# Value preparation on GpSimd per pair of heads, and row-tiled warm-up matmuls, in a fused hash-attention and MLP kernel

## Chip, cores, metric

One core of a Trainium2 chip. The metric is the device time of one launch in microseconds (us). The span of a profile is about 1.8 us shorter than the time of the same run.

## The reference, cut to what matters

```python
def _attn_ref(q, k, v, proj):            # q, k, v: (4, 8, 768, 64)
    q_bits = einsum('bhsd,dk->bhsk', q, proj) > 0      # 6 bits; k_bits likewise
    mask = q_bucket[:, :, :, None] == k_bucket[:, :, None, :]
    scores = where(mask, scale * q @ k.T, -1e9)
    attn = softmax(scores)
    return attn @ v
def _moe_ref(x, w_in, w_out):            # x: (3072, 512), d_ff 2048
    h = x @ w_in
    return (h / (1 + exp(-h))) @ w_out   # silu
```

The kernel does 32 heads in pairs (16 pairs), with 9 score units of 128x512 for each head, and weaves the MLP of a finished batch between later score units.

## The kernel before: the parts concerned

V of each head is cast to float16 (`vv`), and the sum of its six row blocks is made (`vs`). In the first eight heads (and the last) a matmul of `dmat` against `vs` starts the head's output, and the products with `vv` follow; the other heads use `vs` four score units later. A pair's q and k are cast by GpSimd into `qka` (even head) and `qkb` (odd head). `plan(w, fn)` puts work ahead of score unit `w`, in the order of the calls.

```python
    def warm_up(n):
        for _ in range(n):
            nc.tensor.matmul(wps, warm, warm[:, None, :].to_broadcast([P, 4, P]),
                             start=True, stop=True)
    warm_up(5)
    ...                                                   # cut
    def v_unit(p, heads=(0, 1)):
        for i in heads:
            h = 2 * p + i
            vv, vs = VV[h % NVS], VS[p % (NVS // 2)]
            src = v_sb[p][:, i, :].rearrange("p (t d) -> p t d", d=D)
            nc.gpsimd.tensor_copy(out=vv[:, :, 0:D], in_=src)
            sa = nrm.tile([P, 3, D], F32, tag="vsa", name="vsa")
            nc.gpsimd.tensor_tensor(out=sa, in0=src[:, 0:3], in1=src[:, 3:6], op=ALU.add)
            sb = nrm.tile([P, D], F32, tag="vsb", name="vsb")
            nc.gpsimd.tensor_tensor(out=sb, in0=sa[:, 0], in1=sa[:, 1], op=ALU.add)
            nc.gpsimd.tensor_tensor(out=vs[:, i, 0:D], in0=sb, in1=sa[:, 2], op=ALU.add)
    ...                                                   # cut
        # first unit of a head, where direct(h): the first eight heads and the last
            nc.tensor.matmul(o_ps[h][:, 0:NJ, :], dmat,
                             vs[:, None, :].to_broadcast([P, NJ, E1]), start=True, stop=True)
    ...                                                   # cut: start-up
    t_first(0, 0, nc.scalar.copy)             # q_row: TensorE transposes, copy
    t_first(0, 1, nc.vector.tensor_copy)      # k_row
    warm_up(2)
    bt = proj_first(0)                        # projection, bits
    v_unit(0, (0,))
    ...                                                   # cut: casts, bits
    t_first(1, 0, nc.scalar.copy)
    t_first(1, 1, nc.vector.tensor_copy)
    warm_up(3)
    ...                                                   # cut: then the first scores
    for i in range(2):
        plan(8, lambda i=i: cast_unit(1, i))
        plan(8, lambda i=i: v_unit(1, (i,)))
```

The softmax here doesn't subtract the row's maximum and nothing guards it: scores larger than these inputs give would overflow.

Of the kernel before, what the change touches and what calls it, by code (L numbers as in the profile page):

```python
# [9 lines left out]
F32 = mybir.dt.float32  # L10
F16 = mybir.dt.float16
BF16 = mybir.dt.bfloat16
AF = mybir.ActivationFunctionType
ALU = mybir.AluOpType
# [3 lines left out]
def kernel(  # L18
# [10 lines left out]
    nc = tc.nc  # L29
    B, H, S, D = q.shape  # L30
# [3 lines left out]
    P = 128  # L34
    NJ = S // P
# [4 lines left out]
    E1 = D + 1  # L40
# [6 lines left out]
    cst = ctx.enter_context(tc.tile_pool(name="cst", bufs=1))  # L47
# [5 lines left out]
    nrm = ctx.enter_context(tc.tile_pool(name="nrm", bufs=2))  # L53
# [4 lines left out]
    ps = ctx.enter_context(tc.tile_pool(name="ps", bufs=1, space=bass.MemoryType.PSUM))  # L58
# [5 lines left out]
    v_sb = {}  # L64
# [48 lines left out]
    warm = cst.tile([P, P], BF16, name="warm")  # L113
# [7 lines left out]
    wps = ps.tile([P, 4, P], F32, tag="o", name="warm_ps", bufs=2)  # L121

    def warm_up(n):
        for _ in range(n):
            nc.tensor.matmul(wps, warm, warm[:, None, :].to_broadcast([P, 4, P]),
                             start=True, stop=True)

    warm_up(5)
    ident = cst.tile([P, P], F32, name="ident")
    make_identity(nc, ident)  # L130

# [17 lines left out]
    NSL = 4  # L149
    QKA = [cst.tile([P, 2 * S], F16, name=f"qka{i}") for i in range(NSL)]  # L150
    QKB = [cst.tile([P, 2 * S], F16, name=f"qkb{i}") for i in range(NSL)]
    NVS = 8
    VV = [cst.tile([P, NJ, E1], F16, name=f"vv{i}") for i in range(NVS)]
    VS = [cst.tile([P, 2, E1], F16, name=f"vs{i}") for i in range(NVS // 2)]
    for i in range(NVS):
        nc.vector.memset(VV[i][:, :, D:E1], 1.0)
        nc.vector.memset(VS[i // 2][:, i % 2, D:E1], float(NJ))
    for i in range(NSL):
        (nc.vector if i < 2 else nc.gpsimd).memset(QKB[i][0:64, :], 0.0)
    ident16 = cst.tile([P, P], F16, name="ident16")  # L160
# [46 lines left out]
    def cast_first(h, n, e, eng):  # L207
        dst = halves(QKA[0], slice(0, D), n, e) if h == 0 else \
            halves(QKB[0], slice(D, 2 * D), n, e)
        x0 = (2 * h + n) * HS  # L210
        src = qk32[0][e * D : (e + 1) * D, x0 : x0 + HS].rearrange("d (x c) -> d x c", c=P)
        if eng is nc.scalar:
            eng.mul(dst, src, CS)
        else:
            eng.tensor_scalar(out=dst, in0=src, scalar1=CS, scalar2=1.0,
                              op0=ALU.mult, op1=ALU.mult)

    def proj_first(h):

        bp = ps.tile([P, 512], F32, tag="m", name="bp_ps", bufs=3)  # L220
        for c in range(4):
            e, n = divmod(c, 2)
            x0 = (2 * h + n) * HS
            o = e * (NBIT + 1)
            nc.tensor.matmul(bp[32 * c : 32 * c + 32, 0:HS], pw[:, o : o + 32],
                             qk32[0][:, x0 : x0 + HS], start=True, stop=True)
        bt = btp.tile([P, S], F16, tag="bits", name="bits")
        nc.vector.tensor_scalar(out=bt[:, 0:HS], in0=bp[:, 0:HS],
                                scalar1=sc[:, 0:1], scalar2=sc[:, 1:2],
                                op0=ALU.is_gt, op1=ALU.subtract)  # L230
        return bt
# [20 lines left out]
                                scalar1=CS, scalar2=1.0,  # L252
                                op0=ALU.mult, op1=ALU.mult)

    def v_unit(p, heads=(0, 1)):
        for i in heads:
            h = 2 * p + i
            vv, vs = VV[h % NVS], VS[p % (NVS // 2)]
            src = v_sb[p][:, i, :].rearrange("p (t d) -> p t d", d=D)
            nc.gpsimd.tensor_copy(out=vv[:, :, 0:D], in_=src)  # L260
            sa = nrm.tile([P, 3, D], F32, tag="vsa", name="vsa")
            nc.gpsimd.tensor_tensor(out=sa, in0=src[:, 0:3], in1=src[:, 3:6], op=ALU.add)  # L262
            sb = nrm.tile([P, D], F32, tag="vsb", name="vsb")
            nc.gpsimd.tensor_tensor(out=sb, in0=sa[:, 0], in1=sa[:, 1], op=ALU.add)
            nc.gpsimd.tensor_tensor(out=vs[:, i, 0:D], in0=sb, in1=sa[:, 2], op=ALU.add)

    bits = {}
    CB = 256
# [83 lines left out]
    def parts(w):  # L352
        h, r = divmod(w, NU)
        jp, j = divmod(r, 3)
        if j == 1:
            return h, [(2 * jp, 512, 256, 0), (2 * jp + 1, 512, 256, 256)]
        return h, [(2 * jp + j // 2, 0, 512, 0)]
# [17 lines left out]
    def direct(h):  # L375


        return h < H or h == B * H - 1

    def av(w):  # L380
        h, pts = parts(w)
        vv, vs = VV[h % NVS], VS[h // 2 % (NVS // 2)][:, h % 2, :]
        if w % NU == 0:
            o_ps[h] = ps.tile([P, NJ + 1, E1], F32, tag="o", name="o_ps", bufs=2)



            if direct(h):
                nc.tensor.matmul(o_ps[h][:, 0:NJ, :], dmat,  # L389
                                 vs[:, None, :].to_broadcast([P, NJ, E1]),  # L390
                                 start=True, stop=True)
        if w % NU == 4 and not direct(h):
            nc.tensor.matmul(o_ps[h][:, NJ, :], dmat, vs,
                             start=False, stop=True, skip_group_check=True)
        u = ut.pop(w)
        for jt, c0, n, o0 in pts:
            for i in range(n // P):
                nc.tensor.matmul(o_ps[h][:, c0 // P + i, :],  # L398
                                 u[:, o0 + i * P : o0 + (i + 1) * P], vv[:, jt, :],
                                 start=(not direct(h) and w % NU == 0 and i == 0), stop=True,  # L400
                                 skip_group_check=True)
        if w % NU == NU - 1:
            o = o_ps.pop(h)
            p, par = divmod(h, 2)
            if par == 0:
                x_pr[p] = xpl.tile([P, NJ, P], F16, tag="xpr", name="x_pr", bufs=4)
            if not direct(h):

                osum = nrm.tile([P, NJ, E1], F32, tag="osum", name="osum")
                vsum = nrm.tile([P, 1, E1], F32, tag="vsum", name="vsum")  # L410
                nc.vector.tensor_copy(out=vsum, in_=o[:, NJ : NJ + 1, :])
                nc.vector.tensor_tensor(  # L412
                    out=osum, in0=o[:, 0:NJ, :], in1=vsum.to_broadcast([P, NJ, E1]),
                    op=ALU.add)
                o = osum
            rec = nrm.tile([P, NJ], F32, tag="rec", name="rec")
            nc.vector.reciprocal(out=rec, in_=o[:, 0:NJ, D])  # L417
            (nc.vector if direct(h) else nc.gpsimd).tensor_tensor(  # L418
                out=x_pr[p][:, :, par * D : (par + 1) * D], in0=o[:, 0:NJ, 0:D],
                in1=rec[:, :, None].to_broadcast([P, NJ, D]), op=ALU.mult)  # L420
# [124 lines left out]
    t_first(0, 1, nc.vector.tensor_copy)  # L545
    warm_up(2)
    bt = proj_first(0)
    v_unit(0, (0,))
    for e in range(2):
        for n in range(2):  # L550
            cast_first(0, n, e, nc.scalar)
# [10 lines left out]
    def second_head():  # L562
        bt = proj_first(1)
        for e in range(2):
            for n in range(2):
                cast_first(1, n, e, nc.gpsimd)
                bits_first(bt, 1, n, e, nc.vector.tensor_copy)
        v_unit(0, (1,))

    at = {}  # L570

    def plan(w, fn):
        at.setdefault(w, []).append(fn)
# [4 lines left out]
        plan(4 + 2 * i, lambda i=i: t_unit(1, i))  # L578
    for i in range(2):
        plan(8, lambda i=i: cast_unit(1, i))  # L580
        plan(8, lambda i=i: v_unit(1, (i,)))
    plan(10, lambda: proj_halves(1))
    for i in range(2):
        plan(11 + i, lambda i=i: bits_halves(1, i))
# [9 lines left out]
    for i in range(4):  # L594
        plan(29 + i, lambda i=i: bits_unit((2, 3), i // 2, i % 2))
    for i in range(2):
        for j in range(2):
            plan(18 + 9 * i + 2 * j, lambda p=2 + i, j=j: v_unit(p, (j,)))
        plan(21 + i, lambda p=4 + i: load_qk(p))
    for i in range(4):  # L600
        plan((24, 40, 68, 74)[i], lambda i=i: load_w_in(i))
# [7 lines left out]
    for Q in range(2, NQUAD):  # L609
        w0 = (Q - 1) * QST  # L610
        for i in range(4 if Q > 2 else 0):
            w1 = w0 + (5, 9, 12, 15)[i]
            plan(w1, lambda Q=Q, i=i: block_unit(2 * Q + i // 2, i % 2))
            if i % 2:
                for par in range(2):
                    plan(w1, lambda p=2 * Q + i // 2, par=par: cast_unit(p, par))
        wp = w0 + {2: 24, 3: 21}.get(Q, 20)
        plan(wp, lambda Q=Q: proj_unit(2 * Q, 2 * Q + 1))
        for i in range(4):
            plan(wp + {2: i, 3: 2 * i}.get(Q, 0),  # L620
                 lambda Q=Q, i=i: bits_unit((2 * Q, 2 * Q + 1), i // 2, i % 2))
        for i in range(2):
            plan(w0 + 5 + i, lambda p=2 * Q + i: load_v(p))
            for j in range(2):
                plan(w0 + 18 + 9 * i + 2 * j, lambda p=2 * Q + i, j=j: v_unit(p, (j,)))
            if Q + 1 < NQUAD:
                plan(w0 + (28 if Q == 3 else 8) + i, lambda p=2 * Q + 2 + i: load_blocks(p))
    for p in range(NPAIR):
# [11 lines left out]
    for w in range(NW):  # L640
# [9 lines left out]
        n = -(-(len(moeq) - keep) // left) if len(moeq) > keep else 0  # L650
# [6 lines left out]
        if n == 1 and len(moeq) - keep < left and skip:  # L657
            n = 0
# [43 lines left out]
```

## Time and profile before

| | before |
|---|---|
| time, median of the runs beside the changed kernel | 303.59 us (303.19 to 303.80) |
| span of the profile | 301.3 us |
| busy: TensorE, ScalarE, VectorE, GpSimd | 98%, 70%, 60%, 43% |
| first exponential on ScalarE | 8.26 us |
| last eviction's end to the end of the span | 2.5 us |

The prediction shows the page's lines. Two marks are used throughout to compare profiles: when ScalarE's first exponential starts, and how far later exponentials lie behind those of before.

### The profile page before, as it was taken

Reading aid. Unit: us, or ns where it says so; the run is one execution under the profiler, and the core shown is the slowest. Engines: PE = TensorE matmul, PEld = TensorE weight load, DVE = VectorE, ACT = ScalarE, POOL = GpSimd, SP = SyncE. Lnnn points to the kernel's source line nnn. Section 1 sums busy time; section 2 is a strip of 40 time slices with the busy share of each in tenths; the row PEclk is TensorE's granted clock in tenths of the full one; section 3 lists DMA queues with packets and bytes.
Section 4 is the critical chain, followed back from the end, with each engine's and each line's share of the span. In section 5 each row is a group of like instructions: output and inputs, shape, how many; then the busy total and the mean of one; then the engine's idle time right before and its main releaser. Section 6 shows DMA issues by size and latency. Waiting matters only on the chain.

```text
span 301.3 us, 7181 instructions
## 1 busy us (share of the span) xinstructions
PE 296.6 (98%) x2710; PEld 175.1 (58%) x2710; DVE 180.1 (60%) x344; ACT 210.1 (70%) x392; POOL 128.3 (43%) x203
## 2 busy tenths in 40 slices
PE   8999999999999999999999999999999999999996
PEld 3676855545665665555565665555566654446653
DVE  5797938899588355854694434954443443664332
ACT  5987989989886777778876666978977722452200
POOL 7589999388418551935158401755111100000000
PEclk9999999999999999999999999999999999999999
DMA  7999997999988638834078135011022003001112
GB/s 202 243 237 199 181 153 115 199 212 173 150 187 145 107 102 211 126 84 133 3 139 133 49 74 189 2 42 31 2 61 63 20 21 93 35 2 70 37 68 71
DMA packets 103170, 32.87 MB, mean 109 GB/s; under 512 B 90656, under 2 KB 100192, under 8 KB 103136
## 3 DMA queue, kind: packets, MB, share of 16 engines
q1 hardware_dynamic: 98752, 28.22, 44.6%
q0 software_dynamic: 4224, 4.19, 9.0%
q8 instruction: 21, 0.34, 0.5%
q14 instruction: 13, 0.11, 0.1%
q10 hardware_dynamic: 160, 0.00, 0.0%
HBM read 27.27 MB, written 6.29 MB: 111 GB/s over the span
## 4 chain that ended last, share of the span: by engine, by line
PE 88%; DVE 7%; DMA 1%; ACT 1%; issue 1%; SPq 1%; DVEq 0%; ACTq 0%
PE o_ps L496 26%; PE h_ps L461 24%; PE s_ps L366 19%; PE o_ps L398 12%; DVE g L470 3%; PE bp_ps L281 3%; PE tp_ps L185 2%; DMA k_row<-in_k_dram 1%; PE o_ps L482 1%; DVE qk L246 1%; DVE qka L343 1%; ACT u L369 1%; DVE osum L412 1%; SPq L79 0%; PE o_ps L389 0%
## 5 line engine op out<-in xcount | busy, mean ns | idle before, releaser
L369 ACT ACTIVATE u<-s_ps 128x512 f16<-128x512 f32 x288 | 157.0, 606 | 38.7 <-PE s_ps L366 38.3
L470 DVE SCALAR_TENSOR_TENSOR g<-th,h_ps 128x512 f16<-128x512 f32 x96 | 65.5, 687 | 73.8 <-ACT th L468 73.8
L461 PE MATMUL h_ps<-xT,win 128*128 128x512 f16 (+1 forms) x512 | 98.4, 325 | 0.1
L398 PEld LDWEIGHTS <-u 128*128 128x128 f16 x1152 | 68.1, 98 | 42.2 <-ACT u L369 8.4
L496 PE MATMUL o_ps<-wout,g 128*128 128x512 f16 x368 | 91.6, 379 | 0.0
L398 PE MATMUL o_ps<-vv,u 128*128 128x65 f16 x1152 | 82.6, 194 | 0.5 <-ACT u L369 0.4
L468 ACT ACTIVATE th<-h_ps 128x512 f32<-128x512 f32 x96 | 57.9, 603 | 35.9 <-PE h_ps L461 33.2
L461 PEld LDWEIGHTS <-win 128*128 128x128 f16 x512 | 49.9, 98 | 30.5 <-issue 0.4
L418 POOL TENSOR_TENSOR x_pr<-osum,rec 128x384 f16<-128x384 f32 x23 | 19.0, 826 | 88.5 <-DVE rec L417 88.0
L496 PEld LDWEIGHTS <-g 128*128 128x128 f16 x368 | 35.8, 98 | 33.7
L366 PE MATMUL s_ps<-qka 71*128 71x512 f16 x192 | 52.7, 327 | 0.0
L366 PE MATMUL s_ps<-qkb 128*128 128x512 f16 x192 | 52.6, 326 | 0.0
L251 POOL TENSOR_SCALAR qka<-qk 64x1536 f16<-64x1536 f32 x15 | 22.0, 1466 | 11.5 <-DVE qk L246 5.7
L501 DVE TENSOR_SCALAR osb<-o_ps 128x512 f32<-128x512 f32 x23 | 15.9, 691 | 15.0 <-PE o_ps L496 15.0
L251 POOL TENSOR_SCALAR qkb<-qk 64x1536 f16<-64x1536 f32 x15 | 22.1, 1471 | 1.2
L262 POOL TENSOR_TENSOR vsa<-v_sb 128x192 f32<-128x192 f32 x32 | 18.9, 591 | 0.0
L260 POOL CAST vv<-v_sb 128x384 f16<-128x384 f32 x32 | 16.2, 507 | 1.0 <-DMA v_sb<-in_v_dram 0.6
L246 DVE STREAM_TRANSPOSE qk<-k_blk 128x768 f32<-128x768 f32 x10 | 15.8, 1582 | 0.3 <-issue 0.3
L246 DVE STREAM_TRANSPOSE qk<-q_blk 128x768 f32<-128x768 f32 x10 | 16.0, 1596 | 0.0
L366 PEld LDWEIGHTS <-qka 71*128 71x128 f16 x192 | 15.5, 97 | 0.4 <-ACT qka L238 0.3
L366 PEld LDWEIGHTS <-qkb 128*128 128x128 f16 x192 | 15.4, 97 | 0.0
L412 DVE TENSOR_TENSOR osum<-o_ps,vsum 128x390 f32<-128x390 f32 x23 | 13.0, 565 | 2.3
(70 smaller groups left out, 162.5 us busy)
## 6 DMA issues: line engine op xcount, KB each, us to landing
out_dram<-osb SPq DMA_DIRECT2D x23, 256.0 KB
v_sb<-in_v_dram SPq DMA_DIRECT2D x15, 384.0 KB
q_blk<-in_q_dram SPq DMA_DIRECT2D x40, 96.0 KB
k_blk<-in_k_dram SPq DMA_DIRECT2D x40, 96.0 KB
win<-in_moe_w_in_dram POOLq DMA_DIRECT2D x4, 512.0 KB, 7.7
wout<-in_moe_w_out_dram POOLq DMA_DIRECT2D x4, 512.0 KB, 6.2
q_sb<-in_q_dram SPq DMA_DIRECT2D x5, 384.0 KB
k_sb<-in_k_dram SPq DMA_DIRECT2D x5, 384.0 KB
```

The costliest lines, as they stand in the source:

```text
L246: nc.vector.transpose(out=dst, in_=qk_sb[p, "qk"[n]])
L251: nc.gpsimd.tensor_scalar(out=dst[rows, :], in0=qk32[p][rows, :], scalar1=CS, scalar2=1.0, op0=ALU.mult, op1=ALU.mult)
L260: nc.gpsimd.tensor_copy(out=vv[:, :, 0:D], in_=src)
L262: nc.gpsimd.tensor_tensor(out=sa, in0=src[:, 0:3], in1=src[:, 3:6], op=ALU.add)
L366: nc.tensor.matmul(sp[:, o0 : o0 + n], t[rows, S + jt * P : S + (jt + 1) * P], t[rows, c0 : c0 + n], start=True, stop=True)
L369: nc.scalar.activation(out=u, in_=sp, func=AF.Exp, scale=ESC)
L398: nc.tensor.matmul(o_ps[h][:, c0 // P + i, :], u[:, o0 + i * P : o0 + (i + 1) * P], vv[:, jt, :], start=(not direct(h) and w % NU == 0 and ...
L418: (nc.vector if direct(h) else nc.gpsimd).tensor_tensor(out=x_pr[p][:, :, par * D : (par + 1) * D], in0=o[:, 0:NJ, 0:D], in1=rec[:, :, Non ...
L461: nc.tensor.matmul(hp[:, j, :], w_in16[:, dt, ft * P : (ft + 1) * P], xT[4 * b + dt][:, c0 : c0 + n], start=(dt == 0), stop=(dt == NDT - 1))
L468: nc.scalar.activation(out=th, in_=hp, func=AF.Tanh, scale=0.5)
L470: after.append(lambda: nc.vector.scalar_tensor_tensor(out=g[ci][:, grp * f : (grp + 1) * f, :], in0=th, scalar=1.0, in1=hp, op0=ALU.add, o ...
L496: nc.tensor.matmul(o2[tt], g[ci][:, ft, ct * P : (ct + 1) * P], w_out16[:, ft, :], start=(ft == 0), stop=(ft == NFT - 1))
```

## The change

The intent is fewer fixed costs on GpSimd, by preparing both heads of a pair in one instruction, and warm-up matmuls in row tiles in place of some full ones. The diff, cut to its core (the tile shapes, the memsets and the other `plan` calls follow suit):

```diff
-    warm_up(5)
+    def warm_rows(size, n):
+        banks = [ps.tile([P, 2, P], F32, tag="s", name="warm_s", bufs=3) for _ in range(3)]
+        banks.append(wps[:, 0:2, :])
+        for _ in range(n):
+            for r in range(P // size):
+                w = warm[size * r : size * (r + 1)]
+                nc.tensor.matmul(banks[r], w, w[:, None, :].to_broadcast([size, 2, P]),
+                                 start=True, stop=True)
+    warm_up(1)
+    warm_rows(32, 2)
+    warm_up(1)
+    warm_rows(64, 2)
+    warm_up(1)
@@
-    def v_unit(p, heads=(0, 1)):
-        for i in heads:
+    def v_unit(p, heads=slice(0, 2)):
+        n = heads.stop - heads.start
+        vv, vs = VV[p % NVS][:, heads], VS[p % NVS][:, heads]
+        src = v_sb[p][:, heads].rearrange("p h (t d) -> p h t d", d=D)
+        nc.gpsimd.tensor_copy(out=vv[:, :, :, 0:D], in_=src)
+        sa = nrm.tile([P, n, 3, D], F32, tag="vsa", name="vsa")
+        nc.gpsimd.tensor_tensor(out=sa, in0=src[:, :, 0:3], in1=src[:, :, 3:6], op=ALU.add)
         ... (cut)
@@
     for i in range(2):
         plan(8, lambda i=i: cast_unit(1, i))
-        plan(8, lambda i=i: v_unit(1, (i,)))
+    plan(8, lambda: v_unit(1))
```

Besides merging, the last hunk reorders. Before, pair 1's V of the even head came between the two casts; now both casts come first.

More of the change, by code (lines that the diff above doesn't have):

```diff
@@ L151 @@
     QKB = [cst.tile([P, 2 * S], F16, name=f"qkb{i}") for i in range(NSL)]
-    NVS = 8
-    VV = [cst.tile([P, NJ, E1], F16, name=f"vv{i}") for i in range(NVS)]
-    VS = [cst.tile([P, 2, E1], F16, name=f"vs{i}") for i in range(NVS // 2)]
+    NVS = 4
+    VV = [cst.tile([P, 2, NJ, E1], F16, name=f"vv{i}") for i in range(NVS)]
+    VS = [cst.tile([P, 2, E1], F16, name=f"vs{i}") for i in range(NVS)]
     for i in range(NVS):
-        nc.vector.memset(VV[i][:, :, D:E1], 1.0)
-        nc.vector.memset(VS[i // 2][:, i % 2, D:E1], float(NJ))
+        nc.vector.memset(VV[i][:, :, :, D:E1], 1.0)
+        nc.vector.memset(VS[i][:, :, D:E1], float(NJ))
     for i in range(NSL):
@@ L253, in cast_unit @@
                                 op0=ALU.mult, op1=ALU.mult)
-    def v_unit(p, heads=(0, 1)):
-        for i in heads:
-            h = 2 * p + i
-            vv, vs = VV[h % NVS], VS[p % (NVS // 2)]
-            src = v_sb[p][:, i, :].rearrange("p (t d) -> p t d", d=D)
-            nc.gpsimd.tensor_copy(out=vv[:, :, 0:D], in_=src)
-            sa = nrm.tile([P, 3, D], F32, tag="vsa", name="vsa")
-            nc.gpsimd.tensor_tensor(out=sa, in0=src[:, 0:3], in1=src[:, 3:6], op=ALU.add)
-            sb = nrm.tile([P, D], F32, tag="vsb", name="vsb")
-            nc.gpsimd.tensor_tensor(out=sb, in0=sa[:, 0], in1=sa[:, 1], op=ALU.add)
-            nc.gpsimd.tensor_tensor(out=vs[:, i, 0:D], in0=sb, in1=sa[:, 2], op=ALU.add)
+    def v_unit(p, heads=slice(0, 2)):
[5 more added lines that the diff above has]
+        nc.gpsimd.tensor_tensor(out=sa, in0=src[:, :, 0:3], in1=src[:, :, 3:6], op=ALU.add)
+        sb = nrm.tile([P, n, D], F32, tag="vsb", name="vsb")
+        nc.gpsimd.tensor_tensor(out=sb, in0=sa[:, :, 0], in1=sa[:, :, 1], op=ALU.add)
+        nc.gpsimd.tensor_tensor(out=vs[:, :, 0:D], in0=sb, in1=sa[:, :, 2], op=ALU.add)
     bits = {}
@@ L381, in av @@
         h, pts = parts(w)
-        vv, vs = VV[h % NVS], VS[h // 2 % (NVS // 2)][:, h % 2, :]
+        vv, vs = VV[h // 2 % NVS][:, h % 2], VS[h // 2 % NVS][:, h % 2, :]
         if w % NU == 0:
@@ L547 @@
     bt = proj_first(0)
-    v_unit(0, (0,))
+    v_unit(0, slice(0, 1))
     for e in range(2):
@@ L567, in second_head @@
                 bits_first(bt, 1, n, e, nc.vector.tensor_copy)
-        v_unit(0, (1,))
+        v_unit(0, slice(1, 2))
     at = {}
@@ L596 @@
     for i in range(2):
-        for j in range(2):
-            plan(18 + 9 * i + 2 * j, lambda p=2 + i, j=j: v_unit(p, (j,)))
+        plan(18 + 9 * i, lambda p=2 + i: v_unit(p))
         plan(21 + i, lambda p=4 + i: load_qk(p))
@@ L623 @@
             plan(w0 + 5 + i, lambda p=2 * Q + i: load_v(p))
-            for j in range(2):
-                plan(w0 + 18 + 9 * i + 2 * j, lambda p=2 * Q + i, j=j: v_unit(p, (j,)))
+            plan(w0 + 18 + 9 * i, lambda p=2 * Q + i: v_unit(p))
             if Q + 1 < NQUAD:
```

## The prediction

> **What bounds the kernel now.** I read the page first, from its busy times to the chain that ended last, then the timeline of the first 26 us, then the form-by-form table of GpSimd.
>
> ```profile
> PE 296.6 (98%) x2710; PEld 175.1 (58%) x2710; DVE 180.1 (60%) x344; ACT 210.1 (70%) x392; POOL 128.3 (43%) x203
> ...
> POOL 7589999388418551935158401755111100000000
> ...
> PE 88%; DVE 7%; DMA 1%; ACT 1%; issue 1%; SPq 1%; DVEq 0%; ACTq 0%
> ```
>
> TensorE is busy 98% of the span and holds 88% of the chain that ended last. GpSimd is on none of that chain, so what it saves is worth nothing by itself. Its row of slices is the warning: over its whole span it is 43% busy, but in slices 3 to 6 (about 22 to 53 us) it is 90% busy or more. There, and just before, the order of its work can matter even though its sum does not.
>
> The changed warm-up matmuls lie in the first 3.4 us. The timeline of that stretch, TensorE's and the weight loads' lines, then the chain's lines for the same part:
>
> ```profile
> 1.00 0.13 PEld L125 LDWEIGHTS <-warm 128*128 128x128 bf16 x2 [1.00 <-POOL warm L114]
> 1.01 2.32 PE L125 MATMUL warm_ps<-warm 128*128 128x512 bf16 x5 [1.01 <-POOL warm L114]
> ...
> 3.33 0.50 PEld L198 LDWEIGHTS tp_ps<-ident,q_row 128*128 128x128 f32 x3 [0.92 <-issue]
> ...
> 7.79 0.48 PEld L366 LDWEIGHTS <-qka 71*128 71x128 f16 x4 [0.28 <-ACT qka L238]
> ```
>
> ```profile
> 2.96 3.81 DMA k_row<-in_k_dram
> 6.77 0.04 issue
> 6.81 0.55 PE tp_ps L198 x3
> 7.36 0.65 PE warm_ps L125 x3
> 8.01 0.23 PE s_ps L366
> ```
>
> The five old warm-ups start about 0.42 us apart (1.01, 1.41, 1.83, 2.26, 2.69), so the last is through the array near 2.69 + 0.43 = 3.12. The first weight load of the q_row transposes comes at 3.33, though weight loads elsewhere run ahead of the running matmul. So I read 3.33 as the arrival of q_row, not the end of the warm-up, and the warm-up as having about 0.2 us of slack. After that two chains run nearly level: the second head's k_row transfer (landed 6.77, on the path), and transposes, projection, bits, qka copies, which release the first score's weights at 7.79, just before TensorE would be free at 8.01.
>
> The stretch where the GpSimd change can touch the path is pair 1. These are the timeline's lines of GpSimd, and then of ScalarE and TensorE:
>
> ```profile
> 14.83 1.47 POOL L251 TENSOR_SCALAR qka<-qk 64x1536 f16<-64x1536 f32 x1 [2.68 <-DVE qk L187]
> 16.36 0.51 POOL L260 CAST vv<-v_sb 128x384 f16<-128x384 f32 x1
> 16.83 0.59 POOL L262 TENSOR_TENSOR vsa<-v_sb 128x192 f32<-128x192 f32 x1
> 17.50 0.32 POOL L264 TENSOR_TENSOR vsb<-vsa 128x64 f32<-128x64 f32 x1
> 17.90 0.32 POOL L265 TENSOR_TENSOR vs<-vsb,vsa 128x64 f16<-128x64 f32 x1
> 18.31 1.47 POOL L251 TENSOR_SCALAR qkb<-qk 64x1536 f16<-64x1536 f32 x1
> ```
>
> ```profile
> 16.19 9.54 ACT L369 ACTIVATE u<-s_ps 128x512 f16<-128x512 f32 x18 [0.64 <-PE s_ps L366]
> ```
>
> ```profile
> 19.73 0.33 PE L389 MATMUL o_ps<-vs,dmat 128*128 128x390 f16 x1
> ```
>
> The vs that the third head's first matmul (19.73) reads is ready at 17.90 + 0.32 = 18.22: 1.5 us of slack. ScalarE runs its exponentials without a gap, 9.54 / 18 = 0.53 us each, so it is as tight as TensorE here.
>
> [...]591 ns at 192 elements and 320 at 64 make (591 - 320) / 128 = 2.12 ns an element[...] and 185 ns fixed.[...] warm-ups 0.42 us apart at first, and the two at 4.54 take 0.59 together, which is one of 0.38 plus a spacing of 0.21.
>
> **The change part by part.**
> 1. Warm-ups. Removed are two full matmuls of 0.43 us at the early rate. Added are two rounds of four 32-row matmuls and two of two 64-row ones, 256 columns each, so 0.21 us alone. If tiles of a round overlap fully, four rounds cost 4 x 0.21 = 0.85 us, just what the two removed cost. If they do not overlap at all, it is 12 x 0.21 = 2.56, or 1.7 us more.[...] I take 0.1 to 0.4 us longer, of which 0.2 is hidden before q_row lands: +0.1 us on the path. A warm-up that ends sooner gains nothing, since q_row and then k_row set the time.
>
> 2. VectorE's sixteen small memsets become eight larger ones, at 2.1 to 2.4 us. VectorE then has nothing to do on the path until 4.74. Worth 0.
>
> 3. GpSimd's merging, apart from order. Per pair, eight instructions become four. One-input slope from the table: (1466 - 507) / (1536 - 384) = 0.83 ns an element. Merged: cast of 768 elements 507 + 320 = 827 ns, vsa of 384 elements 591 + 407 = 998, vsb and vs of 128 elements 456 each: 2.74 us, against 2 x (507 + 591 + 320 + 323) = 3.48. That is 0.74 us a pair and, over the 15 pairs merged (pair 0 stays split), 11 us less busy time on GpSimd: 128.3 becomes about 117. None of it on the path, as the chain says.
>
> 4. GpSimd's order at pair 1. Before: qka cast, V of head 2, qkb cast, V of head 3. The listing of the changed program has qka cast, qkb cast, then V of both heads. The start stays at 14.83, as it waits for VectorE's copy. Two casts at 1.54 us from start to start put the V copy at 17.91. From starts in the old rows (0.47, 0.67, 0.40) plus the added elements, the new steps are 0.79, 1.08 and 0.54, and the last takes 0.46: vs is ready at 17.91 + 2.87 = 20.78. TensorE asks for it at 19.73. So TensorE stalls for 1.05 us, where it had 1.5 us to spare.
>
> Does that reach the end? At 19.73 scores are issued up to three units ahead. ScalarE, at 0.53 us a unit from 16.19 (unit 13), finishes unit 20 at 16.19 + 8 x 0.53 = 20.43, and unit 21's score, issued behind the stalled matmul, came at 20.01 to 20.39: just in time before, so ScalarE loses all of the stall. It has no gap until 25.73 to make it up, and the projection after it is TensorE's. Perhaps 0.1 to 0.2 us returns from the short waits of TensorE for ScalarE near 22.1. I count +0.9 us.
>
> 5. GpSimd's order later. Pair 2's vs comes at about 29.1 by the same sum (VectorE's copy a microsecond later), for a head that starts at 30.8 plus the delay; pair 3's at 36, for 39.7. No stall. From pair 4 on V is ready far ahead. Weight transfers that GpSimd issues near 51 us come a little sooner; nothing waits for them.
>
> Sum: 303.56 + 0.1 + 0.9 = 304.6 us.
>
> **The rivals.**
> - The stall is absorbed. If ScalarE's backlog or TensorE's own slack covers it, or the merged instructions are much faster than their slopes say, the time stays at 303.5. For it: elsewhere TensorE waits often for ScalarE. Against: unit 21 came just in time, and the merged steps would have to be a third shorter.
> - The row tiles do not overlap. Then the warm-up ends 1.7 us later, at about 4.8; the first transposes, the bits and the first score slip by 1.5, and with the stall the time is 306. For it: no run shows overlap.[...]
> - GpSimd's lighter load frees VectorE, which holds the chain from 55 to 76 us.[...] a gain of up to 1 us is possible there and the time would be 303.6 or a bit less. Against: the same elements are moved, only the fixed part per instruction goes.
>
> **Range and chances.** I give the stall some 75%, 304.3 to 304.9; absorbed, or paid for elsewhere, 15%, 303 to 304; slow row tiles 10%, 305.5 to 306.2. The three runs of before spread by 0.6 us. So 304.6, and 303.3 to 305.9. Two per cent is 6.1 us, which no part comes near: within 2% 0.97, faster 0.01, slower 0.02.
>
> **What would show it right or wrong.** GpSimd busy near 117 us in some 60 fewer instructions; a cast of 768 elements near 827 ns and vsa of 384 near 1 us. In the timeline, TensorE's third dmat matmul waiting for vs on GpSimd for about 1 us near 20 us, and a gap of ScalarE of the same length from about 20.4; the first of the scores at about 7.8 to 8.0. Wrong: no such wait, or a gap that is made up before 55 us; q_row's transposes starting clearly after 3.6; or a different clock of TensorE in the first 8 us.

The sum came to 303.56 + 0.1 + 0.9 = 304.6 us. The 0.1 to 0.4 us, and the 0.1 us that the sum has of it, stand as the author's estimate. The 0.21 us for 256 columns alone is an estimate too, half of the 0.43 us at which the matmuls of 512 columns follow one another. That weight loads run ahead is seen in the same stretch of before: the fifth warm-up's load starts at 2.26 us, its matmul at 2.69.

## More of the kernel before

All runs counted here are of the fast state, in which the share of TensorE's clock that the profile shows as granted is 1.000 in nearly all profiles (0.998 at least).

One caution: the profile of before has a span near the shortest on record for that kernel (301.34 us; the spans of its runs go from 301.2 to 303.1), so a cost of the start, which varies from run to run, looks large against it.

## The result, and the profile after

The changed kernel takes 305.67 us (median; 305.21 to 305.75) against 303.59 us: 1.0073 times, 95% interval 1.0059 to 1.0087. The ratios are those of the fast runs of both kernels; they are close to the ratio of the medians quoted, but not the same (305.67 over 303.59 is 1.0069). The profile is 2.5 us longer, 303.8 against 301.3. The page's busy line and its chain by engine, after:

```profile
PE 297.7 (98%) x2720; PEld 175.3 (58%) x2720; DVE 180.1 (59%) x336; ACT 210.1 (69%) x392; POOL 118.3 (39%) x143
...
PE 84%; DVE 6%; DMA 4%; POOL 3%; issue 1%; ACT 0%; SPq 0%; DVEq 0%; POOLq 0%; ACTq 0%
```

GpSimd does 10 us less work in 60 fewer instructions, and yet it now holds 3% of the chain that ended last, where it held none. Less work, but some of it is now waited for. The 4% of DMA is a transfer, k_blk, that lands near 63 us; the exponentials fall no further behind there, so in this run it adds no delay.

**Near 20 us.** The timeline of the kernel after: GpSimd's work for pair 1, and then what TensorE and ScalarE waited for. A row's last bracket is the idle time before it and what ended it.

```profile
17.33 1.47 POOL L264 TENSOR_SCALAR qkb<-qk 64x1536 f16<-64x1536 f32 x1
18.87 0.83 POOL L272 CAST vv<-v_sb 128x768 f16<-128x768 f32 x1
19.65 1.00 POOL L274 TENSOR_TENSOR vsa<-v_sb 128x384 f32<-128x384 f32 x1
20.73 0.45 POOL L276 TENSOR_TENSOR vsb<-vsa 128x128 f32<-128x128 f32 x1
21.27 0.46 POOL L277 TENSOR_TENSOR vs<-vsb,vsa 128x128 f16<-128x128 f32 x1
21.78 0.33 PE L401 MATMUL o_ps<-vs,dmat 128*128 128x390 f16 x1 [0.93 <-POOL vs L277]
22.54 5.25 ACT L381 ACTIVATE u<-s_ps 128x512 f16<-128x512 f32 x10 [1.23 <-PE s_ps L378]
```

The V work starts only after the second cast, and vs is done at 21.73. TensorE was free 0.93 us before; ScalarE's run of exponentials, unbroken from 16.19 to 25.73 before, now breaks for 1.23 us. The exponentials lay 0.96 us behind those of before ahead of this point and lie 2.05 behind after it: 1.09 us lost here.

**The first 9 us.** TensorE's timeline of the kernel after:

```profile
1.00 0.61 PE L125 MATMUL warm_ps<-warm 128*128 128x512 bf16 x1 [1.00 <-POOL warm L114]
...
2.09 0.61 PE L125 MATMUL warm_ps<-warm 128*128 128x512 bf16 x1
...
2.63 0.61 PE L134 MATMUL warm_s<-warm 64*128 64x256 bf16 x4
...
3.17 0.61 PE L125 MATMUL warm_ps<-warm 128*128 128x512 bf16 x1
...
3.57 0.84 PE L211 MATMUL tp_ps<-ident,q_row 128*128 128x128 f32 x3
...
4.90 1.06 PE L125 MATMUL warm_ps<-warm 128*128 128x512 bf16 x2
```

From the first full warm-up to the second 1.09 us pass, which is one full matmul (0.43), two rounds of 32-row tiles (2 x 0.21) and 0.24 over, which I put down to the two changes of mode between them (128 rows, 32, and 128 again). The single step shows the same: 0.55 us from the first full matmul to the first 32-row tiles, where full ones follow one another at 0.43. So the whole warm-up is four changes, 0.48 us, longer than five full matmuls (its last full one starts at 3.17, that of before at 2.69), and the q_row transposes start at 3.57 instead of 3.36. Something more is lost: the two warm-ups at 4.90 take 1.06 together, where those of before took 0.59. Here TensorE still ran at half rate: the two start 0.43 us apart, those of before 0.21. (The granted clock doesn't show this: the profile has it at 1.00 in these microseconds too. The rate is read from how closely matmuls follow one another.) The first exponential comes at 9.21, 0.95 later than before.

**The end.** The last eviction in the timeline of before, and in that of after:

```profile
298.54 0.29 DVE L485 TENSOR_SCALAR osb<-o_ps 128x128 f32<-128x128 f32 x1 [0.34 <-PE o_ps L482]
```

```profile
300.59 0.29 DVE L497 TENSOR_SCALAR osb<-o_ps 128x128 f32<-128x128 f32 x1 [0.33 <-PE o_ps L494]
```

It ends 2.51 us before the end of the span in the kernel before (301.34) and 2.93 before it in the kernel after (303.81). So 0.42 us are lost once all computing is done. This I had not seen coming.

The three add up: 0.95 + 1.10 + 0.42 = 2.47 us, the difference of the two spans.

### The profile page after: what moved, and what is told of

Its sections match the earlier page's. It is cut to its first block, busy times and chain, and to the rows that moved or that the text cites. A ratio compares the mean times of both kernels' runs of the same rounds, so it can differ in the third digit from the quotient of the medians.

```text
span 303.8 us, 7137 instructions
## 1 busy us (share of the span) xinstructions
PE 297.7 (98%) x2720; PEld 175.3 (58%) x2720; DVE 180.1 (59%) x336; ACT 210.1 (69%) x392; POOL 118.3 (39%) x143
## 4 chain that ended last, share of the span: by engine, by line
PE 84%; DVE 6%; DMA 4%; POOL 3%; issue 1%; ACT 0%; SPq 0%; DVEq 0%; POOLq 0%; ACTq 0%
PE o_ps L508 26%; PE h_ps L473 23%; PE s_ps L378 16%; PE o_ps L410 10%; DMA k_blk<-in_k_dram 4%; PE bp_ps L293 3%; DVE g L482 2%; PE tp_ps L198 1%; PE o_ps L494 1%; PE warm_ps L125 1%; DVE qka L355 1%; POOL vsa L274 1%; POOL qkb L228 0%; POOL qkb L264 0%; POOL qka L264 0%
## 5 line engine op out<-in xcount | busy, mean ns | idle before, releaser
L274 POOL TENSOR_TENSOR vsa<-v_sb 128x384 f32<-128x384 f32 (+1 forms) x17 | 16.1, 949 | 0.0
L272 POOL CAST vv<-v_sb 128x768 f16<-128x768 f32 (+1 forms) x17 | 13.4, 788 | 1.0 <-DMA v_sb<-in_v_dram 0.7
```

The source lines that it names most:

```text
L274: nc.gpsimd.tensor_tensor(out=sa, in0=src[:, :, 0:3], in1=src[:, :, 3:6], op=ALU.add)
```

## The experiments

The theory at this point: the order at pair 1, a longer warm-up and perhaps a later full rate. The rivals were that merged instructions cost time elsewhere too (contention with VectorE), that everything was lost at the start, or that the late full rate was chance. The 0.42 us of the tail, the stretch from the last eviction's end to the end of the span, was found while reading the first four runs. All outputs are right.

### 1. The merge alone

```diff
 changed kernel, but
-    warm_up(1); warm_rows(32, 2); warm_up(1); warm_rows(64, 2); warm_up(1)
+    warm_up(5)
```

> The merged V preparation alone, with the old five warm-ups. Two-cost theory: the third head's first matmul waits for vs on GpSimd about 1.05 us, the first score stays at 7.8 us, and the time is 1.0 to 1.1 us above before (304.6). Rival, all of the loss is from GpSimd (order and contention with VectorE): 2.1 us above (305.7). Rival, all from the start: 303.6.

304.72 us against 303.26: 1.0049 (1.0037 to 1.0061). The wait is there again, and ScalarE's break of 1.23 us with it. TensorE's line:

```profile
20.91 0.33 PE L388 MATMUL o_ps<-vs,dmat 128*128 128x390 f16 x1 [0.93 <-POOL vs L264]
```

The exponentials lie 0.10 us behind before ahead of it and 1.19 after it. That is 1.1 us, but the time is 1.5 above. The last eviction's end is 2.93 us from the end of the span, as in the kernel after. So the order explains most of the merge's cost, and the tail the rest.

### 2. The warm-ups alone, twice

```diff
 kernel before, but
-    warm_up(5)
+    warm_up(1); warm_rows(32, 2); warm_up(1); warm_rows(64, 2); warm_up(1)
```

> The new warm-ups alone, with the old V preparation. Two-cost theory: the first score at about 8.8 us instead of 7.84 (0.2 us from a longer warm-up, the rest from TensorE still at half rate until after 6 us), no wait for vs near 20 us, and 0.9 to 1.0 us above before (304.5). Rival, the late full rate in the profile of after was chance[...]: only the 0.2 us of length, 303.8. Rival, all from the start: 305.7.

> The new warm-ups alone once more. Length theory: 0.3 to 0.6 us above before (1.001 to 1.002), the q_row transposes at 3.57. If the effect was chance, below 1.0005.

303.77 us, 1.0020 (1.0007 to 1.0033), and 303.60 us, 1.0006 (0.9982 to 1.0031): pooled by means, 0.36 us above before (0.52 and 0.20, with a standard error of some 0.2), and not 0.95. The two-cost theory (304.5) failed; its rival of a short delay (303.8) held. The q_row transposes start at 3.57 both times, the first exponential at 8.70 and 8.59. The tail is 2.50 both times. So the start of the kernel after, 0.95 us late in its profile, was partly chance. The second set of runs was too scattered to settle this small cost by times alone.

### 3. The merge in the old order

```diff
 kernel of experiment 1, but
-    for i in range(2):
-        plan(8, lambda i=i: cast_unit(1, i))
-    plan(8, lambda: v_unit(1))
+    plan(8, lambda: cast_unit(1, 0))
+    plan(8, lambda: v_unit(1))
+    plan(8, lambda: cast_unit(1, 1))
```

> Merged V, old warm-ups, and pair 1's V put between its two casts. Order theory: vs ready near 19.2 us, before it is asked for at 19.73; the wait is gone and the time is that of before, 303.4 to 303.7. Rival, the merged instructions themselves cost time (contention, later x_pr): it stays 0.5 us or more above before.

The timeline of this kernel, GpSimd's last step for vs and TensorE's use of it:

```profile
18.80 0.46 POOL L264 TENSOR_TENSOR vs<-vsb,vsa 128x128 f16<-128x128 f32 x1
...
19.77 0.33 PE L388 MATMUL o_ps<-vs,dmat 128*128 128x390 f16 x1
```

vs is ready at 19.26, 0.5 us ahead of its use, and the wait is gone: exponentials lie 0.04 us behind before at the start, and 0.04 to 0.07 all the way to the last unit. So the order was the cause of the wait, and in this profile the merged instructions cost nothing and gained nothing elsewhere: the rival of contention falls in both directions. But the time, 303.83 us, is still 1.0021 (1.0007 to 1.0035), which by itself is what the rival had foretold (0.5 us or more). The span is 0.34 us longer, 0.27 of it in the tail (2.78 us). The profiled run is the fastest of the six (303.45), and where the slower ones lost more isn't recorded.

### 4. The tail

GpSimd takes part in the closing sequence: in the traces of before and after, a drain of it and then its clearing of the semaphores come 0.52 and 0.39 us before the end of the span in before, 0.65 and 0.39 in after. The timeline leaves such instructions out; the trace has them. From the start of the drain's barrier step to the clearing 0.21 or 0.22 us pass in before and in every kernel with the old V, and 0.50 to 0.65 in the merged ones of experiments 1, 3, the kernel after and its repeat. In the view of transfers, the last two microseconds of experiments 1 and 3 show a packet of queue q14, which the view lists as an instruction queue (13 packets and 0.11 MB in the span of before, about 8 KB each). The trace doesn't say whose: between two of its packets GpSimd ran anything from 1 to 40 instructions in before. The line of experiment 3 (that of experiment 1 differs only in its share, 1.1%):

```profile
q14 instruction: 1, 0.01, 1.2%
```

The kernel before has none after 239 us. My theory was that the packet is GpSimd's and holds up its last few instructions, now that sixty fewer have moved its stream. To test the theory I moved the stream on without taking work back:

```diff
 kernel of experiment 3, and
+    pad = cst.tile([P, 1], F32, name="pad")
+    for i in range(8):
+        plan(NW - 20, lambda: nc.gpsimd.memset(pad, 0.0))
```

> The reordered merge with eight one-column memsets more on GpSimd at about 225 us, where it idles; they do nothing but move its later instructions on in its instruction stream. Tail theory: with V merged,[...] holds the closing sequence about 0.33 us (from GpSimd's closing drain to its clearing of semaphores 0.42 us, against 0.13 before); with the pad[...] that step is 0.13 again, the stretch from the last eviction's end to the end of the span is 2.5 us and not 2.8, and the time is that of before within 0.2. Rival, the 0.6 us that the reordered merge lost is not in the tail: it stays at 1.002.

The late packet is gone (there is a new one at 215.8 us, 7 us before the eight memsets run at 223.0), the closing step is 0.21 us (0.12 counted from the drain itself, as in the expectation) and the tail 2.49. The time is 303.72 us, 1.0008 (0.9986 to 1.0030), which holds both "no loss" and the old 1.002, so for the size of the gain the trace counts and not the clock. One thing is not as I wrote: the packet is recorded 0.4 to 0.7 us after the pause has ended, so it isn't what GpSimd waited for. Pause and packet come together (four profiles of four) and go together (all the others), and the pad, which touches GpSimd's stream alone, takes both away, here and in experiment 6. So where that stream stands decides the pause. What fills the pause, and why the new packet comes ahead of the memsets, isn't shown.

This profile also showed what chance does. It has the same five full warm-ups as experiment 3, and the same program until far past 200 us. The two warm-ups after the first transposes, in experiment 3 and here:

```profile
4.61 0.60 PE L125 MATMUL warm_ps<-warm 128*128 128x512 bf16 x2
```

```profile
4.64 1.06 PE L125 MATMUL warm_ps<-warm 128*128 128x512 bf16 x2
```

One run was at full rate by then and the other was not: the eight projections that follow took 1.13 us in the first and 1.36 in the second, whose first exponential came at 9.04 instead of 8.30. So the late full rate needs no row tile. Further on, VectorE waited in this run for a transfer that the other had in time:

```profile
63.26 1.57 DVE L246 STREAM_TRANSPOSE qk<-k_blk 128x768 f32<-128x768 f32 x1 [0.56 <-DMA k_blk<-in_k_dram]
```

The delay behind before grew from 0.77 to 1.44 us there. These two, 0.74 and 0.67 us, are of the size of the 1.7 us over which the six runs of this kernel spread.

### 5. Length of the warm-up, or row tiles?

> Old V, six full warm-ups instead of five: the warm-up lasts 2.56 us in place of 2.13, about as long as the row-tiled one (2.60), with no row tiles. If only the length costs, the q_row transposes start near 3.57 as in after, and the first score slips by 0.9 us (304.5). If the late full rate is what costs, the full rate comes at about 4.3 us as before, and the slip is at most 0.2 us (303.6 to 303.8).

> The same row-tile rounds, but without the first full warm-up, so that the whole warm-up ends at about 3.1 us, as with five full ones. Old V. Length theory: the q_row transposes start at 3.33 to 3.4 and the time is that of before (1.000, within 0.1%). Row-tile theory[...]: the full rate still comes after 5.5 us, the first exponential at 8.6 or later, and the time stays 0.3 to 0.6 us above before.

> Ten rounds of four 32-row tiles and nothing else as the first warm-up, about 2.1 us, old V. Length theory: as before, 1.000. Row-tile theory: the full rate comes much later[...]: after 6.5 us, the first exponential at 9 us or later, and 0.8 us or more above before.

> Nine full warm-ups instead of five, old V: 1.7 us longer at the early rate, so the q_row transposes start at about 4.6 to 4.8 in place of 3.36. Length theory: the first exponential slips by 0.9 to 1.5 us and so does the end (1.003 to 1.005), less what a full rate that has come by then saves. Rival, the length of the warm-up is hidden behind the second head's k_row transfer: below 1.001.

> Four full warm-ups instead of five, ending at 2.7 us, before q_row lands. If q_row's landing sets the transposes and the warm-up has slack, they stay at 3.3 and the time at that of before (within 0.1%); if the warm-up held them, they come up to 0.4 us sooner. If the shorter burst delays the full rate on average, 1.001 or more.

Each is the kernel before with one other first warm-up:

```diff
-    warm_up(5)
+    warm_up(6)                                                      # six full
+    warm_rows(32, 2); warm_up(1); warm_rows(64, 2); warm_up(1)      # rows trimmed
+    warm_rows(32, 10)                                               # rows only
+    warm_up(9)                                                      # nine full
+    warm_up(4)                                                      # four full
```

| first warm-up | q_row transposes | first exponential | time, us | ratio to before (95%) |
|---|---|---|---|---|
| five full (before) | 3.36 | 8.26 | 303.26 to 303.55 | 1 |
| six full | 3.54 | 8.57 | 303.69 | 1.0013 (1.0000 to 1.0025) |
| nine full | 4.70 | 9.05 | 303.97 | 1.0019 (0.9999 to 1.0040) |
| four full | 3.35 | 9.16 | 303.71 | 1.0002 (0.9984 to 1.0019) |
| rows trimmed | 3.37 | 8.56 | 304.00 | 1.0019 (0.9997 to 1.0041) |
| rows only | 3.27 | 8.49 | 303.42 | 0.9995 (0.9975 to 1.0014) |

Six full matmuls, without any row tile, last about as long as the new warm-up and cost about as much (0.4 us), less than half of the 0.9 us that I had expected of length; the time lies in the band that I had given to a late full rate (303.6 to 303.8). Ten rounds of 32-row tiles and nothing else cost nothing that their times show. So nothing shows that row tiles do worse.

But length isn't shown to be the whole of the 0.36 us. With the rows trimmed the transposes start as before, and the first exponential is still 0.30 us late, about as late as with six full ones (0.31). There the full rate came late: the pair of full warm-ups after the transposes took 1.02 us, where it took 0.59 in before and 0.77 with six full ones (the two are full-size matmuls, so a longer pair means the half rate lasted longer). In the second run of the new warm-ups it took only 0.64, and with the transposes 0.21 us late the first exponential was 0.33 late. So either, a longer warm-up or a later full rate, costs about 0.3 us here, and how the 0.36 divides between them stays open.

Nine full ones make the transposes 1.3 us later but the end only 0.79 us in the profile, because the transposes then run at full rate: its three of q_row take 0.49 us instead of 0.87. I had expected 1.003 to 1.005; it is 1.0019. With four, the transposes wait for the transfer, which shows that the warm-up of before had slack until then:

```profile
3.35 0.87 PE L198 MATMUL tp_ps<-ident,q_row 128*128 128x128 f32 x3 [0.45 <-DMA q_row<-in_q_dram]
```

Its late first exponential (9.16) is again a late full rate. The times of the trimmed rows are inconclusive: the median is 0.5 us above before, as the row-tile theory had it, but one of the six runs took 305.32 us, and the interval holds 1. One profile a kernel cannot say whether some warm-ups make a late full rate more likely. That stays open.

In the kernel of row tiles only, the timeline shows how tiles of one round overlap (the four tiles of one round, and one of the next):

```profile
1.62 0.42 PE L134 MATMUL warm_s<-warm 32*128 32x256 bf16 x3
1.63 0.42 PE L134 MATMUL warm_ps<-warm 32*128 32x256 bf16 x1
...
1.84 0.42 PE L134 MATMUL warm_ps<-warm 32*128 32x256 bf16 x1
```

The four start within 0.01 us, and rounds follow at 0.21 us, half of the 0.43 us at which full 512-column matmuls follow one another. So four tiles of 256 columns take no longer than I estimate for one: the overlap is full. All ten rounds follow without a gap; the gaps of 0.12 us are seen only where the mode changes.

### 6. The changed kernel again, and mended

```diff
 changed kernel, and (mended only)
-    for i in range(2):
-        plan(8, lambda i=i: cast_unit(1, i))
-    plan(8, lambda: v_unit(1))
+    plan(8, lambda: cast_unit(1, 0))
+    plan(8, lambda: v_unit(1))
+    plan(8, lambda: cast_unit(1, 1))
+    (and the pad of experiment 4)
```

> The changed kernel once more, beside the same runs of before. Theory: 1.0 to 1.1 us of wait for vs, 2.8 to 2.9 us of tail, first exponential anywhere from 8.6 to 9.3 us[...], 1.006 to 1.007 of before. Rival, its late first exponential (9.21) was of its own making: again 9.2 or later, and 1.0075 or more.

> The whole change, with pair 1's V between its casts and the eight-memset pad: two of the three costs taken away. Three-cost theory (order 1.1 us, tail 0.35 us, warm-up length 0.4 us): no wait for vs near 20 us, 2.5 us from the last eviction to the end, and 303.3 + 0.4, that is 1.001 to 1.002 of before, and 1.6 us below the kernel after. Rival, the parts do not add: more than 1.003.

Again: 305.44 us against 303.55, 1.0062 (1.0042 to 1.0082). Its first exponential comes at 8.59, the wait costs 1.10 us, the tail is 2.94. Only the start differs from the first profile, as chance would have it.

Mended: 303.71 us, 1.0000 (0.9979 to 1.0020), with a tail of 2.50 us and no wait for vs; its profile has a late full rate (9.13) and 0.3 us of waiting for k_blk. With two of three costs taken away, 1.7 us of the loss are gone by the mean of its runs. What is left, the 0.36 us of warm-up, is below what these runs can tell from 0. It does not beat the kernel before.

## Why the prediction was right or wrong

The direction was right and the measured time lay in the range, but the sum was 1.0 us and the measured difference 2.1. That 305.67 us lay in the range was luck: it is above the band given to the stall alone (304.3 to 304.9, 75%), and inside that of slow row tiles (305.5 to 306.2, 10%), a rival that is false. Of the signs named, the wait near 20 us and GpSimd's times came true; the first score at 7.8 to 8.0 us did not (8.80, and 8.18 in the repeat), and the other rate of TensorE in the first 8 us, named as a sign of being wrong, was seen. By its steps:

1. **Warm-ups, +0.1 us: too small.** The warm-up's lengthening was above what I gave (0.48 us against 0.1 to 0.4), by the four changes of mode at 0.12 us each, which I had not sized. The tiles themselves overlap fully, so what I had added for a partial overlap was not lost. The slack of 0.2 us was right (four full matmuls wait for q_row). So 0.21 us came through at the transposes, where I had 0.1. One reading was off here: the chain's view lets the first score begin at 8.01, but in the timeline its matmul starts at 7.84, right after its weights. The cost in time is 0.36 us by the mean of twelve runs, with some 0.2 of error. The further 0.6 us in the first profile are chance, since the repeat of the same kernel has its first exponential at 8.59 instead of 9.21; the range ought to have carried this. With the same five full warm-ups it fell at 8.26, 8.30, 8.35 and 9.04.
2. **VectorE's memsets, 0: right,** as far as the profiles show: nothing waits for them.
3. **The merged instructions: right.** Here are the groups of GpSimd by form, after, against the 998 and 827 ns that were predicted:

```profile
L274 POOL TENSOR_TENSOR vsa<-v_sb 128x384 f32<-128x384 f32 x15 | 15.0, 997 | 0.0
L272 POOL CAST vv<-v_sb 128x768 f16<-128x768 f32 x15 | 12.4, 826 | 0.3
```

4. **The order at pair 1, +0.9 us: the mechanism right, the size 1.10.** vs came 2.86 us after the V cast's start against 2.87 predicted. The 0.1 to 0.2 us that I let come back did not: the exponentials fall behind by 1.09 us at unit 21 and by no less at any later one. My working had it (1.05); the deduction for short waits was a guess, and it was wrong.
5. **The order later, 0: right** up to the last unit. But "None of it on the path" missed a cost that has nothing to do with work: 0.42 us in the closing sequence, which experiment 4 ties to where the shorter stream of GpSimd's instructions ends.

With the measured terms the sum is 1.10 + 0.42 + 0.36 = 1.88 us, against 2.2 and 1.9 us in the two comparisons of the whole change (0.0073 and 0.0062 of 303.6).

Of the rivals, absorption was refuted by the unbroken delay in experiment 1, slow row tiles by the rows-only kernel, and a gain for VectorE by experiment 3, where nothing was won from 55 to 76 us (the delay behind before did not fall there).

## What to carry to other kernels

Merging instructions of an engine that is off the critical path bought nothing here by itself, and it cost: a merged unit delivers its first half only when the second is done, and whatever moved ahead of it delays both (pair 1's vs was ready at 21.73 us here, the even head's at 18.22 before). So list for each consumer when it asks and when its producer is done, and keep the order of the tightest pair when merging. When two versions differ by a few tenths of a percent, compare the offsets of matching instructions along the whole program and at its very end: where times scatter by a microsecond, the offsets still tell one cost from another. A cost at the start is the exception: it varied by 0.7 us between equal programs, so it takes several profiles.
